# MLP steps of one width (512 columns) and a new written-out issue order, in a kernel for windowed attention and two MLP layers

## The chip, the cores and the metric

The kernel runs on one core of a Trainium2 chip. Times are device microseconds (us). The kernel before takes 620.37 us (median of 3 runs, 620.18 to 620.58). One profiled execution took 622.03 us, of which its trace spans 620.2 us. TensorE is called PE below (PEld is its weight load), VectorE DVE, ScalarE ACT, GpSimd POOL, and the queue that starts the DMAs is SyncE's, SP.

## What is computed

Attention over 2 batches, 8 heads, 768 tokens and head size 64, and then two MLP layers over all 1536 tokens (d_model 512, d_ff 2048):

```
k_sum = max of k, v_sum = mean of v over blocks of 32 tokens (24 blocks)
scores = concat(q k^T / 8 where |i-j| < 16, else -1e9;  q k_sum^T / 8 + log 32)
x = softmax(scores) @ concat(v, v_sum)            -> 1536 tokens x 512
h = x @ w_in ;  y = (h * clip(h+3, 0, 6) / 6) @ w_out      layer 0
h = y @ w_in2;  out = (h * sigmoid(h)) @ w_out2            layer 1
```

All of it is float32. For the MLPs every operand is split in a high and a low part, and each product is three matmuls: high by high, high by low, low by high.

## The kernel before

**Attention.** A unit is 64 query tokens of one batch, all 8 heads; there are 24. A unit goes through `keys` (the 96 near keys and 24 block maxima are copied together, on POOL or DVE), `scores` (PE), `masked` (DVE: adds the mask, finds the maximum), `exps` and `guard` (ACT), `inverse` (DVE), `normal` (POOL or DVE), `turn` (PE transposes), `turned` (copy), `mix` (PE, times the values), `mixed_hi` and `mixed_lo` (the two parts of x). Ahead of that, k and q come in tiles of 256 tokens: `load`, `par` (a copy that puts even and odd tokens apart, one half on DVE and one on ACT), `tr` (PE transposes, two per tile), `k_copy`, `k_max`, `q_copy` out of PSUM. All block maxima of a batch must be there before its first `keys`.

**Weights.** Each of 64 half slices of weights (512 KB) is fetched and rounded to its high and low part: `conv_mag` (ACT), `conv_low`, `conv_clamp`, `conv_join`, `conv_sign` (DVE), `conv_hi` (ACT or DVE), `conv_lo` (POOL or DVE).

**MLP.** The hidden dimension is cut into 16 slices of 128, eight in each half of a layer. A step is one slice f for one chunk of tokens: `hidden i` (12 matmuls in two parts of 6), `act` (ACT), `gate` (DVE), `gate_hi`, `gate_lo` (the two parts of the gated values), `project i` (12 matmuls into 4 PSUM banks, which gather the chunk's output over eight steps). Chunks are 512 tokens (`WIDE`). Only the first chunk of layer 0, half 0 has eight steps of 256 tokens among its steps: slices 0 to 3, each for the tokens of units 0 to 3 and for those of units 4 to 7. So the kernel before has 100 steps. There are 8 PSUM banks in turn, one buffer for `act`'s result (`r`; two more come with `grow 4`), two for the gated values (`g`).

**What sets the order.** The string `ORDER` is the whole program, about 1800 entries, one call each; every engine runs its own share of it strictly in that order, and a `*` puts an operation on DVE that would else be on ACT or POOL. Waits between engines follow from the tiles. `rouse` and `warm` are matmuls whose results nobody uses.

Of the kernel before, what the change touches and what calls it, by code (L numbers as in the profile page):

```python
# [87 lines left out]
1, load k 1 0, k_copy 0 1 0, tr k 0 2 0, k_max 0 2 0, q_copy 0 0 0 1*, tr q 0 2 1, q_copy 0 2 1 0, tr q 0 2 0,
warm 10, par k 0 0, k_max 0 2 1, par k 0 1, tr k 0 0 1, k_copy 0 0 1, tr k 0 0 0, k_max 0 0 1, q_copy 0 2 1 1,
k_copy 0 0 0, tr k 1 0 0, conv_lo 1, k_copy 0 2 0, table 1, warm 0, tr k 1 0 1, q_copy 0 2 0 1, k_max 0 0 0,  # L90
keys 3, k_copy 1 0 1, k_copy 1 0 0, k_max 1 0 0, k_max 1 0 1, fetch 2, conv_low 2, scores 3, masked 3, keys 1,
scores 1, masked 1, keys 2, conv_mag 2, conv_clamp 2, exps 3, guard 3, exps 1, scores 2, keys 0, scores 0,
# [5 lines left out]
7, keys 11, scores 11, guard 7, normal 0, load v 0 2, v_sums 0 2, v_add 0 1, inverse 2, turn 0, exps 5, guard
5, normal 2, load k 1 2, conv_sign 3, v_add 0 2, v_rows 0, conv_join 3, v_put 0 1, turned 0*, v_add 1 0,
load_v 1, tr k 1 2 1, k_copy 1 2 1, k_max 1 2 1, keys 4, scores 4, v_put 0 0*, inverse 5, v_put 0 3, turn 2,  # L100
turned 2, tr k 1 2 0, k_copy 1 2 0, inverse 7, masked 4, k_max 1 2 0, mix 1, v_put 0 2, exps 4, guard 4,
conv_lo 2, keys 9, load k 1 1, mixed_hi 1*, mixed_lo 1, scores 9, tr k 1 1 1, load_v 0, tr k 1 1 0, k_copy 1 1
0, masked 6, normal 5, exps 6, k_max 1 1 1, turn 5, k_copy 1 1 1*, keys 8, guard 6, fetch 4, conv_low 4,
conv_sign 4, mix 0, mixed_hi 0*, mixed_lo 0, scores 8, inverse 6, k_max 1 1 0, turned 5, inverse 4, keys 10,
scores 10, load_v 2, mix 2, conv_mag 4, conv_clamp 4, load_v 3, mixed_hi 2, mixed_lo 2, unstage, normal 7, mix
3, mixed_hi 3, mixed_lo 3, turn 7, turned 7, normal 6, turn 6, conv_hi 3, conv_lo 3, turned 6, conv_join 4,
conv_hi 4, load q 1 0, hidden 0 0, hidden 0 1, act 0, masked 9, tr q 1 0 1, masked 10, q_copy 1 0 1 0, q_copy
1 0 1 1*, tr q 1 0 0, q_copy 1 0 0 1, fetch 5, conv_mag 5, hidden 1 0, hidden 1 1, conv_lo 4*, hidden 2 0,
q_copy 1 0 0 0, act 1, gate 0, gate_hi 0, load q 1 2, tr q 1 2 1, conv_low 5, conv_sign 5, q_copy 1 2 1 0,
gate 1, gate_hi 1, conv_clamp 5, conv_join 5, keys 13, scores 13, q_copy 1 2 1 1, normal 4, turn 4, tr q 1 2  # L110
0, turned 4, fetch 6, conv_low 6, conv_mag 6, keys 12, q_copy 1 2 0 0, conv_sign 6, q_copy 1 2 0 1, conv_clamp
6, conv_join 6, conv_hi 5, masked 11, gate_lo 0, gate_lo 1, conv_hi 6, hidden 2 1, conv_lo 6, project 0 0,
project 1 0, load_v 4, mix 4, mixed_hi 4, mixed_lo 4, act 2, load_v 6, mix 6, gate 2, mixed_hi 6, mixed_lo 6,
load_v 5, mix 5, masked 8, mixed_hi 5, mixed_lo 5, exps 9, guard 9, load_v 7, mix 7, hidden 3 0, hidden 3 1,
act 3, project 0 1, project 1 1, mixed_hi 7*, mixed_lo 7, gate_hi 2*, hidden 5 0, hidden 5 1, gate 3, gate_hi
3*, inverse 9, conv_lo 5, keys 15*, fetch 8, conv_low 8, gate_lo 3*, exps 10, gate_lo 2, guard 10, fetch 7,
conv_mag 7, conv_clamp 7, conv_low 7, conv_sign 7, conv_join 7, hidden 4 0, hidden 4 1, act 5, gate 5, exps 8,
inverse 10, normal 9, guard 8, inverse 8, turn 9, turned 9, project 2 0, project 2 1, hidden 6 0, hidden 6 1,
load_v 9, masked 13, gate_hi 5, conv_hi 7, conv_lo 7*, mix 9, project 3 0, project 3 1, conv_mag 8, conv_clamp
8, conv_sign 8, exps 13, guard 13, mixed_hi 9*, mixed_lo 9, conv_join 8, inverse 13, act 4, gate 4, fetch 11,  # L120
gate_hi 4*, gate_lo 4*, normal 8, turn 8, gate_lo 5, project 5 0, exps 11, guard 11, project 5 1, conv_hi 8*,
turned 8, act 6, gate 6, gate_hi 6, gate_lo 6*, load v 1 1, v_pair 1 1, v_sums 1 1, normal 13, turn 13, turned
13*, hidden 7 0, hidden 7 1, act 7, gate 7, gate_hi 7, scores 12, masked 12, fetch 9, conv_mag 9, conv_low 9,
conv_sign 9, exps 12, project 4 0, conv_clamp 9, guard 12, scores 15, fetch 10, masked 15, exps 15, conv_lo 8,
guard 15, conv_join 9, conv_hi 9*, conv_low 10, conv_sign 10, hidden 8 0, hidden 8 1, load q 1 1, inverse 12,
normal 10, load v 1 2, turn 10, turned 10, gate_lo 7, project 7 0, conv_mag 10, conv_clamp 10, load_v 8, mix
8, project 4 1, act 8, gate 8, inverse 11, keys 14, project 7 1, v_add 1 1, v_pair 1 2, v_sums 1 2, v_add 1 2,
# [834 lines left out]
```

## Time and profile before

| | |
|---|---|
| median of 3 runs | 620.37 us |
| profiled execution | 622.03 us |
| its span in the trace | 620.2 us |
| PE busy | 603.6 us, 97% |
| DVE busy | 406.8 us, 66% |
| ACT busy | 240.3 us, 39% |
| POOL busy | 100.4 us, 16% |
| chain that ended last | PE 90%, DVE 4%, ACT 3%, DMA 1% |

Read the shares by stretch, not over the whole span: the first 120 us hold all of the attention and much of the weight conversion, and there several engines are near full; after that PE alone has no pause. A matmul's listed duration is longer than the distance to the next one, since matmuls overlap; what a matmul costs is the distance from start to start.

### The profile page before, as it was taken

Reading aid. Unit: us, or ns where it says so; the run is one execution under the profiler, and the core shown is the slowest. Engines: PE = TensorE matmul, PEld = TensorE weight load, DVE = VectorE, ACT = ScalarE, POOL = GpSimd, SP = SyncE. Lnnn points to the kernel's source line nnn. Section 1 sums busy time; section 2 is a strip of 40 time slices with the busy share of each in tenths; the row PEclk is TensorE's granted clock in tenths of the full one; section 3 lists DMA queues with packets and bytes.
Section 4 is the critical chain, followed back from the end, with each engine's and each line's share of the span. In section 5 each row is a group of like instructions: output and inputs, shape, how many; then the busy total and the mean of one; then the engine's idle time right before and its main releaser. Section 6 shows DMA issues by size and latency. Waiting matters only on the chain.

```text
span 620.2 us, 8857 instructions
## 1 busy us (share of the span) xinstructions
PE 603.6 (97%) x3324; PEld 506.6 (82%) x3324; DVE 406.8 (66%) x895; ACT 240.3 (39%) x574; POOL 100.4 (16%) x113
## 2 busy tenths in 40 slices
PE   6699999999999999999999999999999999999997
PEld 5688988788888888888888888888888888888886
DVE  5869999876757678567659688435266766423333
ACT  5779967464434224233223243222232243101120
POOL 2564562031102012100003101000000010000000
PEclk9989999999999999999999999999999999999999
DMA  9979393421322223222203222202012220100101
GB/s 250 286 152 238 124 219 91 129 62 45 95 63 98 79 91 94 77 68 63 73 1 102 63 73 73 64 0 70 0 35 81 89 68 1 51 18 1 68 1 68
DMA packets 69050, 51.56 MB, mean 83 GB/s; under 512 B 36368, under 2 KB 63504, under 8 KB 69008
## 3 DMA queue, kind: packets, MB, share of 16 engines
q1 hardware_dynamic: 69008, 51.01, 30.3%
q8 instruction: 26, 0.43, 0.3%
q14 instruction: 16, 0.13, 0.1%
...
## 4 chain that ended last, share of the span: by engine, by line
PE 90%; DVE 4%; ACT 3%; DMA 1%; issue 1%; SPq 0%; POOL 0%; ACTq 0%; POOLq 0%
PE bank L688 41%; PE bank L762 21%; PE bank L759 20%; PE bank L580 3%; PE bank L649 2%; PE bank L637 2%; DMA stage<-in_q_dram 1%; ACT early_w L508 1%; DVE bits L410 1%; DVE bits L403 1%; ACT kT L483 1%; ACT early_w L609 0%; PE bank L524 0%; PE bank L475 0%; DVE bits L390 0%
## 5 line engine op out<-in xcount | busy, mean ns | idle before, releaser
L688 PE MATMUL bank<-x,w 128*128 128x512 f32 (+1 forms) x1008 | 231.3, 381 | 0.4 <-DVE w L425 0.3
L688 PEld LDWEIGHTS bank<-x,w 128*128 128x128 f32 x1008 | 182.6, 188 | 36.3 <-DVE w L425 0.5
L759 PE MATMUL bank<-g,w 128*128 128x512 f32 (+1 forms) x624 | 141.3, 376 | 0.0
L762 PE MATMUL bank<-w,g 128*128 128x512 f32 (+1 forms) x600 | 135.7, 381 | 0.0
L762 PEld LDWEIGHTS bank<-w,g 128*128 128x128 f32 x600 | 109.6, 188 | 21.8
L759 PEld LDWEIGHTS bank<-g,w 128*128 128x128 f32 x624 | 110.3, 188 | 20.7 <-DVE g L736 0.2
L425 POOL TENSOR_TENSOR w<-bits,w 128x512 fp32r<-128x512 f32 x38 | 51.0, 1347 | 353.5 <-ACT w L421 196.7
L736 DVE TENSOR_TENSOR g<-r,g 128x512 fp32r<-128x512 f32 (+1 forms) x95 | 66.9, 709 | 29.2 <-ACT g L730 26.3
L726 DVE TENSOR_TENSOR r<-bank,r 128x512 f32<-128x512 f32 x48 | 32.9, 688 | 65.9 <-ACT r L716 65.7
L716 ACT ACTIVATE r<-bank 128x512 f32<-128x512 f32 x48 | 28.1, 596 | 112.3 <-PE bank L688 109.8
L385 ACT ACTIVATE mag<-words 128x512 f32<-128x512 f32 x64 | 43.0, 671 | 27.6 <-DVE bits L403 20.1
L722 DVE SCALAR_TENSOR_TENSOR r<-r,bank 128x512 f32<-128x512 f32 (+1 forms) x52 | 33.1, 641 | 27.6 <-ACT r L714 27.1
L714 ACT ACTIVATE r<-bank 128x512 f32<-128x512 f32 (+1 forms) x52 | 29.0, 563 | 53.6 <-PE bank L688 42.4
L410 DVE SCALAR_TENSOR_TENSOR bits<-words,bits 128x512 uint32<-128x512 uint32 x64 | 48.5, 758 | 1.3
L403 DVE SCALAR_TENSOR_TENSOR bits<-mag,bits 128x512 uint32<-128x512 uint32 x64 | 47.2, 737 | 1.6
L421 ACT CAST w<-bits 128x512 fp32r<-128x512 f32 x40 | 24.7, 620 | 57.0 <-DVE bits L403 56.9
L688 PE MATMUL bank<-x_late,w 128*128 128x512 f32 x192 | 44.8, 389 | 0.0
L688 PEld LDWEIGHTS bank<-x_late,w 128*128 128x128 f32 x192 | 36.0, 188 | 7.5
L730 ACT CAST g<-r 128x512 fp32r<-128x512 f32 (+1 forms) x43 | 25.4, 594 | 36.0 <-PE bank L762 16.4
L397 DVE TENSOR_SCALAR mag<-mag 128x512 f32<-128x512 f32 x64 | 31.6, 493 | 9.0 <-ACT mag L385 8.8
L730 DVE CAST g<-r 128x512 fp32r<-128x512 f32 (+1 forms) x57 | 28.8, 505 | 11.9 <-PE bank L762 8.3
L609 ACT ACTIVATE early_w<-early_w,stat 128x120 f32<-128x120 f32 x72 | 27.5, 387 | 13.5 <-DVE stat L595 13.5
...
## 6 DMA issues: line engine op xcount, KB each, us to landing
...
```

The lines of the kernel that those rows point to most:

```text
L385: nc.scalar.activation(out=out, in_=low_high(h)[:, 1].bitcast(F32), func=AF.Abs, scale=EXP_SHIFT)
L397: nc.vector.tensor_scalar(out=mag, in0=mag, scalar1=MAG_MIN, scalar2=MAG_MAX, op0=ALU.max, op1=ALU.min)
L403: nc.vector.scalar_tensor_tensor(out=bits, in0=mags.use(h).bitcast(U32), scalar=3, in1=bits, op0=ALU.logical_shift_left, op1=ALU.bitwise_or,)
L410: nc.vector.scalar_tensor_tensor(out=bits, in0=low_high(h)[:, 1], scalar=0x80000000, in1=bits, op0=ALU.bitwise_and, op1=ALU.bitwise_or,)
L425: eng.tensor_tensor(out=w_half(h, 1), in0=bitss.use(h).bitcast(F32), in1=w_half(h, 0).bitcast(F32), op=ALU.subtract,)
L688: nc.tensor.matmul(ps[:, :n], w[:, a, kk * P : (kk + 1) * P], x[:, o // SUB : (o + n) // SUB, b, kk, :], start=(m == 0), stop=(m == last),)
L722: nc.vector.scalar_tensor_tensor(out=r, in0=r, scalar=6.0, in1=ps, op0=ALU.min, op1=ALU.mult)
L726: nc.vector.tensor_tensor(out=r, in0=ps, in1=r, op=ALU.mult)
L730: copier("gate_hi", i)(out=g[:, 0, cols], in_=rs.use(slot(i)[0])[:, cols])
L736: eng.tensor_tensor(out=g[:, 1, cols], in0=r[:, cols], in1=g[:, 0, cols].bitcast(F32), op=ALU.subtract)
L759: nc.tensor.matmul(ps[:, o : o + n], lhs, g[:, b, shift : shift + n], **flags)
L762: nc.tensor.matmul(ps[:, : len(cols)], g[:, a, rows], rhs, **flags)
```

## The change

The eight steps of 256 tokens become four of 512, so that there are 96 steps, and `ORDER` is another string: other places for nearly every entry, other choices of `*`, four `warm` entries for five. Nothing else differs; line numbers fall by 7.

```diff
-FIRST_STEPS = (
-    [(c, 1, f) for c in range(2) for f in range(4)]
-    + [(0, 2, f) for f in range(4, HALF)]
-    + [(c, 2, f) for c in (2, 4) for f in range(HALF)]
-)
+FIRST_STEPS = [(c, 2, f) for c in range(0, 6, 2) for f in range(HALF)]
...
+0, keys 3, conv_clamp 0, q_copy 0 1 0 0, conv_join 0, scores 3, masked 3, exps 0, keys 1*, scores 1, k_copy 0
...
```

The transfers, first. SP's queue at the start of the kernel before (`stage` and `early_w` are tiles of k, q and v, `words` are weights, the first `cst` has the identity, the second the masks):

```order
L433 DMA stage_80<-in_k_dram 128x8x128
L874 DMA cst<-in_consts_dram 128x176
L377 DMA words_69<-in_moe_w_in_dram 128x4x256
L433 DMA stage_81<-in_q_dram 128x8x128
L433 DMA stage_82<-in_k_dram 128x8x128
L377 DMA words_70<-in_moe_w_out_dram 128x1024
L448 DMA early_w_88<-in_q_dram 128x8x64 x2
L433 DMA stage_83<-in_k_dram 128x8x128
L448 DMA early_w_88<-in_k_dram 128x8x64 x2
L874 DMA cst<-in_consts_dram 128x360
```

and the same queue with the change:

```order
L426 DMA stage_80<-in_k_dram 128x8x128
L867 DMA cst<-in_consts_dram 128x176
L426 DMA stage_81<-in_k_dram 128x8x128
L426 DMA stage_82<-in_q_dram 128x8x128
L426 DMA stage_83<-in_k_dram 128x8x128
L441 DMA early_w_88<-in_q_dram 128x8x64 x2
L370 DMA words_69<-in_moe_w_in_dram 128x4x256
L867 DMA cst<-in_consts_dram 128x360
L370 DMA words_70<-in_moe_w_out_dram 128x1024
```

The third k tile of batch 0 was the eighth transfer and is the fifth; the weights have moved behind the tiles of k and q.

DVE next, from its sixth instruction in the kernel before (`bits`, `mag` and `words` belong to the weights' conversion, L461 is `par`, L489 `k_max`, L506 `q_copy`):

```order
L461 COPY stage_81<-stage_81 128x512
L390 TENSOR_SCALAR bits_67<-words_69 128x512
L410 SCALAR_TENSOR_TENSOR bits_67<-words_69,bits_67 128x512
L397 TENSOR_SCALAR mag_66<-mag_66 128x512
L403 SCALAR_TENSOR_TENSOR bits_67<-mag_66,bits_67 128x512
L425 TENSOR_TENSOR w_85<-bits_67,w_85 128x512
L461 COPY stage_82<-stage_82 128x512
L390 TENSOR_SCALAR bits_68<-words_70 128x512
L397 TENSOR_SCALAR mag_66<-mag_66 128x512
L410 SCALAR_TENSOR_TENSOR bits_68<-words_70,bits_68 128x512
L403 SCALAR_TENSOR_TENSOR bits_68<-mag_66,bits_68 128x512
L421 CAST w_85<-bits_68 128x512
```

and with the change, from its seventh (L454 is `par`, L482 `k_max`, L476 `k_copy`, L499 `q_copy`, L588 the first `masked`):

```order
L454 COPY stage_82<-stage_82 128x512
L482 TENSOR_REDUCE kmax_104<-bank_74 128x2x8
L476 COPY kT_98<-bank_75 128x2x256
L482 TENSOR_REDUCE kmax_104<-bank_75 128x2x8
L454 COPY stage_83<-stage_83 128x512
L482 TENSOR_REDUCE kmax_104<-bank_77 128x2x8
L482 TENSOR_REDUCE kmax_104<-bank_73 128x2x8
L499 TENSOR_SCALAR early_w_89<-bank_78 64x8x64
L499 TENSOR_SCALAR early_w_90<-bank_79 64x8x64
L383 TENSOR_SCALAR bits_67<-words_69 128x512
L403 SCALAR_TENSOR_TENSOR bits_67<-words_69,bits_67 128x512
L588 ISA early_w_95,stat_100<-bank_77,cst 128x120
```

Two conversions stood ahead of the first `masked`, and two instructions of one are left there.

Last, PE around its first `hidden` in the kernel before (L649 is `mix`, L637 `turn`, L475 `tr`, L688 `hidden`, L580 `scores`):

```order
L649 MATMUL bank_73<-early_units 64x64 x8
L649 MATMUL bank_78<-early_units 64x64 x8
L637 MATMUL bank_79<-cst,early_units 120x128 x4
L637 MATMUL bank_75<-cst,early_units 120x128 x4
L688 MATMUL bank_73<-x_0_64,w_85 128x256 x12
L475 MATMUL bank_78<-cst,early_w_88 128x128 x4
L475 MATMUL bank_79<-cst,early_w_88 128x128 x4
L688 MATMUL bank_75<-x_0_64,w_86 128x256 x12
```

and with the change (L642 is `mix`, L630 `turn`, L573 `scores`, L681 `hidden`, L468 `tr`):

```order
L642 MATMUL bank_78<-early_units 64x64 x8
L642 MATMUL bank_74<-early_units 64x64 x8
L630 MATMUL bank_75<-cst,early_w_95 120x128 x4
L642 MATMUL bank_73<-early_g_96,early_r_97 64x64 x8
L573 MATMUL bank_77<-early_units,early_w_89 128x120 x4
L681 MATMUL bank_78<-x_0_64,w_85 128x512 x12
L468 MATMUL bank_79<-cst,early_w_88 128x128 x4
L468 MATMUL bank_74<-cst,early_w_88 128x128 x4
L681 MATMUL bank_73<-x_0_64,w_86 128x512 x12
```

The first `hidden` is 512 wide now and stands behind eight `mix` in place of four.

## Rows read from the trace of the kernel before

**Rows 1.** Stretches: length, busy us of PE, PEld, DVE, ACT, POOL, granted clock.

```profile
0.00:52.40 52.40, 40.59 (x369) 36.02 (x369) 37.20 (x130) 36.34 (x111) 23.24 (x44) 0.93 1.00 231
5.06:23.70 18.64, 11.38 (x92) 10.15 (x91) 13.68 (x25) 11.82 (x21) 4.87 (x12) 1.00 1.20 289
23.70:52.40 28.70, 25.20 (x263) 21.86 (x261) 23.35 (x105) 23.23 (x89) 13.89 (x22) 0.88 0.96 207
...
30.00:40.00 10.00, 10.00 (x100) 8.58 (x100) 6.25 (x35) 7.71 (x38) 5.34 (x9) 0.69 0.60 126
50.00:110.00 60.00, 57.69 (x557) 52.13 (x558) 56.42 (x184) 48.17 (x148) 29.65 (x31) 1.00 0.67 160
52.40:80.00 27.60, 25.91 (x271) 24.55 (x272) 25.95 (x85) 23.97 (x78) 14.77 (x16) 1.00 0.65 164
180.00:617.00 437.00, 437.00 (x1977) 362.73 (x1976) 263.47 (x450) 124.22 (x217) 38.26 (x28) 1.00 0.17 55
```

**Rows 2.** Chain that ended last: start, us, what.

```profile
314.71 13.60 PE bank L688 x60
...
603.23 13.86 PE bank L762 x75
```

**Rows 3.** PE in order of time: start, duration, line, shape, count, [idle before].

```profile
9.16 1.17 PE L475 MATMUL bank<-cst,stage 128*128 128x128 f32 x8 [2.23 <-DVE stage L461]
...
20.92 1.15 PE L580 MATMUL bank<-early_units,early_w 128*128 128x120 f32 x8 [1.10 <-POOL early_units L573]
...
24.59 1.04 PE L475 MATMUL bank<-cst,early_w 128*128 128x128 f32 x8
25.46 1.06 PE L880 MATMUL bank<-cst 128*128 128x128 f32 x8
28.65 0.63 PE L637 MATMUL bank<-cst,early_units 128*120 128x128 f32 x4 [2.14 <-DVE stat L624]
...
52.37 1.81 PE L688 MATMUL bank<-x,w 128*128 128x256 f32 x12
...
62.07 0.69 PE L649 MATMUL bank<-early_g,early_r 120*64 120x64 f32 x16
62.59 0.64 PE L649 MATMUL bank<-early_units 120*64 120x64 f32 x16
...
68.11 3.04 PE L688 MATMUL bank<-x,w 128*128 128x256 f32 x24
70.99 0.60 PE L637 MATMUL bank<-cst,early_w 128*120 128x128 f32 x4
...
79.67 0.65 PE L637 MATMUL bank<-cst,early_w 128*120 128x128 f32 x4 [0.76 <-POOL early_w L629]
```

**Rows 4.** DVE in order of time, same columns.

```profile
5.06 0.43 DVE L461 COPY stage<-stage 128x512 f32<-128x512 f32 x1 [4.06 <-DMA stage<-in_k_dram]
...
23.70 0.27 DVE L595 CUSTOM_DVE_ANT_0 early_units<-bank,cst 128x120 f32<-128x120 f32 x1
...
25.32 0.42 DVE L397 TENSOR_SCALAR mag<-mag 128x512 f32<-128x512 f32 x1
...
32.71 0.29 DVE L535 COPY early_w<-bank 128x128 f32<-128x128 f32 x1 [1.81 <-PE bank L524]
```

**Rows 5.** ACT in order of time: `par` of the third k tile, batch 0.

```profile
16.03 0.62 ACT L461 COPY stage<-stage 128x512 f32<-128x512 f32 x1 [0.51 <-DMA stage<-in_k_dram]
```

**Rows 6.** DVE by line and shape: name, count, busy us, mean ns, idle before.

```profile
L489 DVE TENSOR_REDUCE kmax<-bank 128x16 f32<-128x512 f32 x12 | 8.1, 686 | 4.1 <-ACT kT L483 4.1
...
L672 DVE TENSOR_TENSOR x<-bank,x 128x256 fp32r<-128x256 f32 x16 | 6.6, 420 | 1.1 <-ACT x L668 0.7
```

**Rows 7.** Page, the engines' instructions by line, same columns.

```profile
L736 DVE TENSOR_TENSOR g<-r,g 128x512 fp32r<-128x512 f32 (+1 forms) x95 | 66.9, 709 | 29.2 <-ACT g L730 26.3
...
L722 DVE SCALAR_TENSOR_TENSOR r<-r,bank 128x512 f32<-128x512 f32 (+1 forms) x52 | 33.1, 641 | 27.6 <-ACT r L714 27.1
L714 ACT ACTIVATE r<-bank 128x512 f32<-128x512 f32 (+1 forms) x52 | 29.0, 563 | 53.6 <-PE bank L688 42.4
...
L410 DVE SCALAR_TENSOR_TENSOR bits<-words,bits 128x512 uint32<-128x512 uint32 x64 | 48.5, 758 | 1.3
```

More of the change, by code (lines that the diff above doesn't have):

```diff
@@ L88 @@
[L88 to L92, printed above, removed]
@@ L98 @@
[L98 to L102, printed above, removed]
@@ L103 @@
[L103 to L127, printed above, removed]
@@ new lines @@
+7, mix 7, mixed_hi 7, load_v 6, mixed_lo 7, mixed_lo 4, mix 6, mixed_hi 6, turn 9, keys 10, conv_lo 2,
+mixed_lo 6, load_v 5, mix 5, mixed_hi 5, scores 10, mixed_lo 5, fetch 4, conv_low 4, masked 10, conv_hi 3,
+conv_lo 3, k_copy 1 0 1, conv_mag 4, conv_clamp 4, conv_sign 4, turned 9, hidden 0 0, conv_join 4, hidden 0 1,
+exps 8, guard 8, load k 1 2, inverse 8, tr k 1 2 0, k_max 1 2 0, v_add 1 2, tr k 1 2 1, act 0, gate 0, gate_hi
+0*, gate_lo 0, conv_hi 4, hidden 1 0, conv_lo 4*, fetch 5, conv_low 5, conv_sign 5, hidden 1 1, exps 11,
@@ new lines @@
+conv_low 11, gate_lo 4, turned 12, conv_clamp 11, turn 13, conv_sign 11, conv_lo 9*, scores 14, conv_join 11,
+fetch 15, conv_hi 11, conv_low 12, conv_lo 11, conv_mag 12, conv_sign 12, masked 14, turned 13, hidden 5 1,
+masked 15, act 5, gate 5, tr q 1 2 0, q_copy 1 2 0 0, project 4 0, exps 15, guard 15, tr q 1 2 1, grow 0,
+conv_clamp 12, keys 17, gate_hi 5*, gate_lo 5, load_v 13, mix 13, mixed_hi 13, fetch 14, conv_low 14, keys 16,
+q_copy 1 2 1 0, conv_join 12, conv_hi 12, scores 17, q_copy 1 2 1 1, project 5 0, project 5 1, normal 11*,
@@ new lines @@
+12, gate_lo 6, conv_low 15, normal 14, turn 14, turned 14, turn 10, turned 10, conv_sign 15, hidden 7 1,
+masked 16, keys 18*, act 7, mix 14, scores 18, conv_join 15, inverse 17, exps 16, gate 7, conv_hi 15, load_v
+11, mix 11, mix 10, mixed_hi 10, mixed_hi 11, guard 16, conv_hi 13*, conv_lo 13*, project 6 0, project 6 1,
+gate_hi 7*, mixed_lo 10, fetch 16, conv_mag 16, gate_lo 7, conv_lo 15*, project 7 0, load_v 17, finish 0 0 0
+0, finish 0 0 0 1, project 7 1, finish 0 0 0 3, fetch 20, inverse 16, normal 16, conv_low 16, mixed_lo 11,
@@ new lines @@
+17, act 9, gate 9, exps 21, guard 21, hidden 10 0, hidden 10 1, inverse 21, normal 21*, gate_hi 9, gate_lo 9,
+grow 1, turned 18, conv_sign 17, load_v 19, mix 19, conv_mag 17, conv_clamp 17, conv_join 17, conv_hi 17*,
+turn 21, turned 21, mixed_hi 19, mixed_lo 19, hidden 13 0, keys 20, scores 20, masked 20, scores 23, conv_lo
+16*, masked 23, fetch 18, conv_low 18, hidden 13 1, conv_mag 18, act 10, exps 20, exps 23, gate 10, hidden 12
+0, conv_sign 18, guard 20, inverse 20, project 8 0, project 8 1, guard 23, mixed_lo 17, conv_clamp 18,
@@ new lines @@
+conv_join 18, hidden 12 1, conv_lo 17, project 9 0, project 9 1, gate_hi 10, gate_lo 10, keys 22*, scores 22,
+act 11, gate 11, grow 2, conv_hi 18, fetch 19, conv_mag 19, normal 20*, turn 20, conv_low 19, load_v 21,
+load_v 18, masked 22, exps 22, guard 22, project 10 0, mix 18, project 10 1, gate_hi 11*, gate_lo 11, project
+11 0, act 12, gate 12, mix 21, mixed_hi 18*, project 11 1, gate_hi 12*, mixed_lo 18, gate_lo 12, project 12 0,
+inverse 22, act 13, gate 13, gate_hi 13, gate_lo 13, hidden 14 0, hidden 14 1, turned 20*, load_v 20, mix 20,
```

340 lines of the change are left out of this document (173 added, 167 removed).

## The prediction

> **What bounds the kernel now.** I read the page's shares first, then the stretches, the chain that ended last, and PE and DVE in order of time. From 180 us on PE has no pause: 437.0 of 437 us busy at full clock [rows 1]. There the chain is PE alone, in pieces like 60 matmuls in 13.60 us, or 226.7 ns per matmul of 512 columns, up to 603.23 + 13.86 = 617.1 us [rows 2]. So what happens on the other engines there costs nothing, and the end is set by how much matmul work is left when PE stops waiting. Each microsecond that PE loses early is one at the end.
>
> It loses them before its first `hidden` at 52.37 us [rows 3]: `scores` starts only at 20.92, `rouse` and `warm` fill gaps, and the clock falls. From 30 to 40 us the granted clock is 0.69 on average [rows 1]; with the two levels 1.2 and 2.4 GHz that is 6.2 us at the lower one, or 3.1 us of matmul time. From 52.4 to 80 us PE is still idle for 27.60 - 25.91 = 1.7 us [rows 1], the longest pause 0.76 us [rows 3].
>
> Behind PE's waits there stands DVE. Of the first 52.4 us it is busy 37.2 [rows 1]. The 15.2 idle ones are 4.9 until the first tile lands at 5.06, 18.64 - 13.68 = 5.0 from there to the first `masked` at 23.70, and 28.70 - 23.35 = 5.3 after it [rows 1, 4]; of these last the longest pause, 1.81, waits for matmuls at the low clock [rows 4]. From 50 to 110 us DVE is 94% busy (56.42 of 60) [rows 1]: near its limit.
>
> **The change, part by part.** The sum is made against the profiled execution: span 620.2 us, 1.8 more around it (622.03), which I leave as they are; the difference then goes onto the median of 620.37.
>
> *(a) Width.* Eight steps of 24 matmuls with 256 columns become four of 24 with 512. A run of 24 narrow ones goes from 68.11 to 70.99, 120.0 ns each [rows 3]. So 192 x 120.0 = 23.0 us become 96 x 226.7 = 21.8: -1.3 us, all on PE's path. What is saved is a fixed cost: 512 columns at 2.4 GHz are 213.3 ns, the row has 13 more. The Trainium skill ("TensorE: Matmul & The Clock Gate", section "Wait — 56ns, not 53.3ns?") puts it at about 2.5 ns per matmul; by that the saving would be 96 x 2.5 ns = 0.2 us, an estimate. The rows measure this kernel's own pairs of weight load and matmul, so they decide.
>
> *(b) The head.* Three things move. The third k tile of batch 0 was the eighth transfer, reached at 16.03 us [rows 5], and becomes the fifth. Two weight conversions leave the stretch ahead of the first `masked` on DVE. And the first `hidden`, 512 wide, now needs units 0 to 7, not 0 to 3.
>
> First `masked`: at some 2 us per transfer (16.03 / 8) the tile lands at 10 instead of 16 us. In the kernel before 7.7 us pass from the tile to the first `masked`, partly because conversions stand between. With all of the 7.7 it comes at 17.7, without 1.2 us of it at 16.5; I take 17.2. Until then, counted from the first `par`, DVE has 16 instructions in place of 25 that took 13.68 us [rows 1], so 8.8 us: its idle time there is 17.2 - 5.1 - 8.8 = 3.3, not 5.0.
>
> First `hidden`: counted over both orders up to the last `mixed_lo` that it needs, DVE has three `masked` more (two of them take 23.70 to 25.32, 0.81 each [rows 4]: +2.4), four `mixed_lo` more (0.42 each [rows 6]: +1.7) and four `k_max` fewer (0.69 each [rows 6]: -2.8). The rest (a conversion less, two `keys` and a `v_pair` taken over from POOL) I count as even. So 37.2 + 1.3 = 38.5 us of DVE work. Idle: 4.9 + 3.3 + late pauses. Late ones were 5.3, in part the low clock's; the new order has longer attention chains ahead of `hidden`, but more units in flight to fill them. None would be the best, 5.3 the same; I take the middle, 2.7. That gives 38.5 + 4.9 + 3.3 + 2.7 = 49.4 us for the first `hidden`. ACT's share up to there, 36.3 us now [rows 1], changes by two operations and stays below DVE's, and POOL with 23.2 has room.
>
> PE has by then also done more: four `mix` (62.07 to 62.59, 0.52 each [rows 3]) and two `turn` more, four `tr` less (24.59 to 25.46 holds two, 0.44 each [rows 3]; `turn` has as many matmuls): 2.1 + 0.9 - 1.8 = +1.2 us that need not be done later. Gain of the head: 52.4 - 49.4 + 1.2 = 4.2 us. Bounds: no late pause and `masked` at 16.5 give 46.0 and a gain of 7.6; all idle time as before gives 38.5 + 15.2 = 53.7 and a gain of -0.1.
>
> *(c) The first chunk's eight steps.* After the head PE asks for more sooner, and DVE, 94% busy there, has conversions to do that the kernel before had behind it. This loss the trace doesn't show directly. At best the 1.7 us of pauses go (-1.7). At worst each of the eight steps ends with a pause like the longest there now, 0.76 us: +6.1. I take +2.0, nearer the small pauses, because PE has transposes, `scores`, `turn` and `mix` of 16 units to lay between.
>
> *(d) The rest.* Layer 0's later chunks, layer 1 and the last `close` hold the same matmuls in another order. In PE's present 437 us without pause DVE is busy 263 and ACT 124 [rows 1], so moved conversions and DMAs hide. At the end four parts of `project`, 24 matmuls or 5.4 us, lie between the last `hidden` and `close`, over a chain of `act`, `gate`, a cast and `gate_lo` of about 0.6 + 0.6 + 0.6 + 0.7 = 2.5 us [rows 7]. Zero; without that cover it would be those 2.5 us.
>
> Sum: -1.3 - 4.2 + 2.0 = -3.5 us. Span 616.7, profiled execution 618.5, median 620.4 - 3.5 = 616.9 us. With all bounds at one end: 620.4 - 1.3 - 7.6 - 1.7 = 609.8 and 620.4 - 1.3 + 0.1 + 6.1 = 625.3.
>
> **Rivals.**
>
> *Head and first chunk both smooth.* `hidden` at 47, no loss in (c): -1.3 - 5.4 - 1.2 = -7.9, so 612.5 us. For it: DVE's longest pause in the present head follows a slow clock. Against: ACT is busy 36.3 of 52.4 us too, and two engines that loaded, each in strict order, seldom run without waits.
>
> *The clock falls again.* It fell after PE's pause of 2.14 us that ended at 28.65; an earlier one of 2.23, ended at 9.16, was followed by no fall [rows 3, 1]. In the new order `scores 1` waits for `keys 1` on DVE, which stands behind three `masked` and two pieces of a conversion, some 3.6 us, while PE has two `scores` of about 1 us: it will wait about 2 us again. If the clock then halves, the pauses come back, `hidden` starts at 53.7, and the sum is -1.3 + 0.1 + 2.0 = +0.8: 621.2, no change that can be told. The Trainium skill ("TensorE: Matmul & The Clock Gate", section "What's actually happening") says that the low clock is the default and only activity lifts it. The trace agrees for the second pause and not for the first, so I don't take the fall for certain.
>
> *Slower: the single `r` buffer starves PE.* Until `grow 4` there is one buffer for `act`'s result, and the next step's `act` waits for `gate_lo`. At 512 columns that chain is 2.5 us [rows 7], and where DVE puts the pieces of a conversion into it (three at up to 0.76 us [rows 7]) some 4.8. PE's cover per step is the next `hidden`, 2.7 us, and 1 to 2 us of attention. If a step loses 1 us, eight lose 8: -1.3 - 4.2 + 8 = +2.5, so 622.9. It decides from 0.84 us per step on (6.7 in all, which takes the sum to +1.2). Against it: of the 2.3 us that PE idles from 50 to 110 us, 1.7 lie before 80 [rows 1], so at most 0.6 fall where steps of 512 already run on the same buffer.
>
> **How the numbers follow.** Forecast 0.58, own range 614.5 to 619.1; smooth 0.14; clock 0.15; starved 0.13. A difference under 0.2% (1.24 us) is about what can't be told from none. The forecast and the smooth case are faster, and a little of the clock case, where a fall is short: 0.73. The rest of the clock case and the mild end of the starved one make "same" 0.15; slower 0.12. The range reaches from the smooth case to the edge of the starved one: 612.4 to 621.8.
>
> **What would show it.** First `masked` near 17 us, first `hidden` near 49 to 50 and a granted clock of 1.00 up to there would show (b) right; a stretch at 0.50 after the third `scores` would show the second rival. For (c), PE's idle time from the first `hidden` to 110 us: under 4 us for the forecast, over 8 with `act` behind `gate_lo` for the starved case. (a) needs 226.7 ns per matmul in all MLP runs. The forecast is wrong if the first `hidden` comes after 53 us, or if PE pauses anywhere after 180 us.

## The result, and the profile after

The changed kernel takes 612.58 us (median of 4 runs, 612.36 to 613.91) beside 620.48 us for the kernel before: ratio 0.9875, 95% interval 0.9857 to 0.9892, or -7.9 us. Forecast were 616.9 us and -3.5; the time lies inside the range of 612.4 to 621.8 by 0.2 us, the gain is more than twice the forecast one. The profiled execution took 612.76 us, its span is 611.0. A few executions, those profiled for the control and for the twelve doubled signs among them, ran disturbed (859 to 862 us at a granted clock near 0.65 from end to end, or 1363 and 2990 us) and are left out of every median.

The stretches of the changed kernel (columns as in [rows 1]: length, busy us of PE, PEld, DVE, ACT, POOL, granted clock, DMA share, GB/s):

```profile
0.00:52.40 52.40, 45.45 (x457) 39.64 (x458) 42.34 (x171) 40.08 (x135) 30.96 (x46) 0.97 1.09 244
5.06:23.70 18.64, 14.04 (x99) 13.01 (x99) 14.97 (x50) 12.31 (x35) 4.77 (x12) 0.91 1.19 284
23.70:52.40 28.70, 27.40 (x343) 22.62 (x342) 27.20 (x121) 26.48 (x100) 21.71 (x24) 1.00 1.11 233
30.00:40.00 10.00, 9.79 (x143) 8.01 (x143) 9.18 (x39) 9.82 (x38) 8.13 (x10) 1.00 1.09 219
50.00:110.00 60.00, 60.00 (x433) 50.03 (x432) 55.86 (x156) 49.94 (x146) 13.39 (x18) 1.00 0.75 186
52.40:80.00 27.60, 27.60 (x174) 22.84 (x173) 25.48 (x66) 24.70 (x70) 8.61 (x11) 1.00 0.91 217
```

Against [rows 1] every engine does more in the first 52.4 us (DVE 42.3 us for 37.2, POOL 31.0 for 23.2), the clock stays at 1.00 from 30 to 40 us, and from 52.4 to 80 us PE is busy 27.60 of 27.60 us, where it had been 25.91. DVE is as loaded as before there (25.48 for 25.95).

PE in order of time (start, duration, line, shape, count, [idle before and who ended it]), for [rows 3]:

```profile
9.81 0.65 PE L468 MATMUL bank<-cst,stage 128*128 128x128 f32 x4 [0.44 <-DVE stage L454]
11.95 2.15 PE L468 MATMUL bank<-cst,stage 128*128 128x128 f32 x12 [1.48 <-DVE stage L454]
...
16.29 1.05 PE L573 MATMUL bank<-early_w,early_w 128*128 128x120 f32 x8
...
19.30 1.15 PE L573 MATMUL bank<-early_units,early_w 128*128 128x120 f32 x8 [1.06 <-POOL early_units L566]
21.83 2.04 PE L573 MATMUL bank<-early_w,early_w 128*128 128x120 f32 x16 [1.39 <-DVE early_w L566]
...
48.48 2.98 PE L681 MATMUL bank<-x,w 128*128 128x512 f32 x12
51.30 1.03 PE L468 MATMUL bank<-cst,early_w 128*128 128x128 f32 x8
52.09 3.02 PE L681 MATMUL bank<-x,w 128*128 128x512 f32 x12
```

`scores` starts at 16.29 us (20.92 before), the first `hidden` at 48.48 (52.37), and behind it no line has an idle time. The wait for `keys 1`, at which the prediction's rival of the falling clock let it fall, is there (1.39 us ahead of 21.83) and no fall follows it in this execution. A fall stands elsewhere: the twelve transposes behind the pause of 1.48 us take 2.15 us, and from 12.8 to 16.1 us the clock is 0.50:

```profile
12.80:16.10 3.30, 3.30 (x18) 3.30 (x17) 2.46 (x4) 1.67 (x3) 0.93 (x3) 0.50 1.08 371
```

The third k tile on ACT, for [rows 5], and the first `masked` on DVE, for [rows 4]:

```profile
10.94 0.62 ACT L454 COPY stage<-stage 128x512 f32<-128x512 f32 x1 [0.74 <-DMA stage<-in_k_dram]
```

```profile
17.48 0.28 DVE L588 CUSTOM_DVE_ANT_0 early_w<-bank,cst 128x120 f32<-128x120 f32 x1 [0.15 <-PE bank L573]
```

The tile is there at 10.94 us (16.03; 10 forecast), `masked` at 17.48 (23.70; 17.2 forecast). The chain that ended last, for [rows 2], is PE alone from the first `hidden` on, in the same 226.7 ns per matmul (5.44 us for 24) where the MLP's matmuls stand together; one piece ahead of it is new, a transfer of v that PE waits for twice, 0.45 and 0.38 us:

```profile
40.92 5.90 DMA early_r<-in_v_dram
...
243.79 5.44 PE bank L681 x24
```

Three groups of the page, for [rows 7] (count, busy us, mean ns, idle before):

```profile
L729 DVE TENSOR_TENSOR g<-r,g 128x512 fp32r<-128x512 f32 x96 | 66.4, 699 | 28.5 <-ACT g L723 25.4
...
L403 DVE SCALAR_TENSOR_TENSOR bits<-words,bits 128x512 uint32<-128x512 uint32 x64 | 44.7, 698 | 1.0
...
L715 DVE SCALAR_TENSOR_TENSOR r<-r,bank 128x512 f32<-128x512 f32 x48 | 32.5, 683 | 14.0 <-ACT r L707 13.8
```

The operations of a step cost what they cost (0.70 for 0.71 us; 0.68 for 0.68 at 512 columns, since the 0.64 of [rows 7] has eight `gate` of 256 columns among its 52); the waits ahead of them are DVE's and not PE's.

**Where the time went.** A PE that never waits behind its first `hidden` needs a time from there to the end that only its own instructions set. So each trace falls into two parts, the start of the first `hidden` and the rest of the span:

| trace | first `hidden` | rest | span |
|---|---|---|---|
| before | 52.37 | 567.8 | 620.2 |
| after | 48.48 | 562.5 | 611.0 |
| difference | -3.9 | -5.3 | -9.2 |

The 5.3 us of the rest: width -1.3 as forecast; matmuls that now stand ahead of the first `hidden`, by the traces' counts behind it (64 fewer `mix`, 8 `turn` and 16 for the sums of v, 16 more `tr`; at the distances in the trace of before, -2.1 - 0.9 - 0.7 + 1.8) -1.9; pauses -1.7; and -0.4 that these don't explain. The traces differ by 9.2 us and the medians by 7.9, because the profiled execution of before (622.03 us) lay 1.6 us above the median of 620.48 and that of after 0.2 above its own.

### The profile page after: what moved, and what is told of

Read it like the earlier page. It is cut to its first block, busy times and chain, and to the rows that moved or that the text cites. A ratio compares the mean times of both kernels' runs of the same rounds, so it can differ in the third digit from the quotient of the medians.

```text
span 611.0 us, 8649 instructions
## 1 busy us (share of the span) xinstructions
PE 600.7 (98%) x3224; PEld 499.4 (82%) x3224; DVE 402.4 (66%) x912; ACT 240.3 (39%) x570; POOL 67.4 (11%) x84
## 4 chain that ended last, share of the span: by engine, by line
PE 95%; DVE 2%; ACT 1%; DMA 1%; issue 0%; ACTq 0%
PE bank L681 43%; PE bank L752 22%; PE bank L755 21%; PE bank L573 3%; PE bank L642 2%; PE bank L630 1%; PE bank L468 1%; DMA early_r<-in_v_dram 1%; PE bank L883 1%; ACT early_units L602 0%; DVE kmax L482 0%; PE bank L536 0%; PE bank L873 0%; ACT early_w L501 0%; ACT early_w L602 0%; DVE early_w L588 0%
## 5 line engine op out<-in xcount | busy, mean ns | idle before, releaser
L681 PE MATMUL bank<-x,w 128*128 128x512 f32 x960 | 230.8, 391 | 0.0
L681 PEld LDWEIGHTS bank<-x,w 128*128 128x128 f32 x960 | 179.0, 188 | 37.1 <-DVE r L719 0.5
L752 PE MATMUL bank<-g,w 128*128 128x512 f32 x576 | 138.3, 392 | 0.0
L729 DVE TENSOR_TENSOR g<-r,g 128x512 fp32r<-128x512 f32 x96 | 66.4, 699 | 28.5 <-ACT g L723 25.4
L709 ACT ACTIVATE r<-bank 128x512 f32<-128x512 f32 x48 | 27.8, 596 | 119.4 <-PE bank L681 118.9
L418 POOL TENSOR_TENSOR w<-bits,w 128x512 fp32r<-128x512 f32 x23 | 31.5, 1371 | 361.4 <-DVE w L414 218.3
L707 ACT ACTIVATE r<-bank 128x512 f32<-128x512 f32 x48 | 28.5, 597 | 57.8 <-PE bank L681 48.9
L723 ACT CAST g<-r 128x512 fp32r<-128x512 f32 x49 | 30.2, 621 | 48.0 <-PE bank L755 21.7
L403 DVE SCALAR_TENSOR_TENSOR bits<-words,bits 128x512 uint32<-128x512 uint32 x64 | 44.7, 698 | 1.0
L681 PE MATMUL bank<-x_late,w 128*128 128x512 f32 x192 | 45.0, 389 | 0.0
L681 PEld LDWEIGHTS bank<-x_late,w 128*128 128x128 f32 x192 | 36.0, 188 | 7.5
L715 DVE SCALAR_TENSOR_TENSOR r<-r,bank 128x512 f32<-128x512 f32 x48 | 32.5, 683 | 14.0 <-ACT r L707 13.8
L723 DVE CAST g<-r 128x512 fp32r<-128x512 f32 x47 | 20.5, 436 | 18.0 <-PE bank L755 14.0
L418 DVE TENSOR_TENSOR w<-bits,w 128x512 fp32r<-128x512 f32 x41 | 27.9, 689 | 1.5 <-ACT w L414 0.7
```

The lines of the kernel that those rows point to most:

```text
L403: nc.vector.scalar_tensor_tensor(out=bits, in0=low_high(h)[:, 1], scalar=0x80000000, in1=bits, op0=ALU.bitwise_and, op1=ALU.bitwise_or,)
L418: eng.tensor_tensor(out=w_half(h, 1), in0=bitss.use(h).bitcast(F32), in1=w_half(h, 0).bitcast(F32), op=ALU.subtract,)
L681: nc.tensor.matmul(ps[:, :n], w[:, a, kk * P : (kk + 1) * P], x[:, o // SUB : (o + n) // SUB, b, kk, :], start=(m == 0), stop=(m == last),)
L715: nc.vector.scalar_tensor_tensor(out=r, in0=r, scalar=6.0, in1=ps, op0=ALU.min, op1=ALU.mult)
L723: copier("gate_hi", i)(out=g[:, 0, cols], in_=rs.use(slot(i)[0])[:, cols])
L729: eng.tensor_tensor(out=g[:, 1, cols], in0=r[:, cols], in1=g[:, 0, cols].bitcast(F32), op=ALU.subtract)
```

## The experiments

The time given first for each experiment is a median, with the range in brackets; the medians of the kernel before, measured beside them, are 620.6 to 620.9 us. For the changed kernel its seven undisturbed runs are the base: 612.31 to 613.91, median 612.8.

**The width.** Every matmul of layer 0, half 0 of the changed kernel cut in two of 256 columns, 576 more instructions in the same order:

```diff
+            if i < 3 * HALF:
+                for part_n in range(2):
+                    nc.tensor.matmul(
+                        ps[:, part_n * SUB : (part_n + 1) * SUB],
+                        w[:, a, kk * P : (kk + 1) * P],
+                        x[:, part_n, b, kk, :],
...
```

> The changed kernel, with each matmul of the 24 steps of layer 0, half 0 issued as two of 256 columns into the same bank: 576 matmuls become 1152, nothing else changes. By the price of the rows (120.0 ns against half of 226.7) PE needs 576 x 13.3 ns = 7.7 us more: about 620.3. If width costs only some 2.5 ns per matmul (rival), 1.4 us more: about 614.

620.0 us (619.6 to 620.9): +7.2, or 12.5 ns per matmul added. Its first `hidden` and what follows:

```profile
49.69 3.12 PE L683 MATMUL bank<-x,w 128*128 128x256 f32 x24
52.65 1.03 PE L468 MATMUL bank<-cst,early_w 128*128 128x128 f32 x8
```

24 narrow ones take 2.96 us where 12 wide ones took 2.82 (48.48 to 51.30), 11.7 ns per matmul added. Part of the 7.2 us is the clock's: this trace has a fall that costs 1.2 us of first `hidden` (below). Its rest alone, 569.0 us for 562.5, gives 6.5 us or 11.3 ns. The Trainium skill ("TensorE: Matmul & The Clock Gate", section "Wait — 56ns, not 53.3ns?") has about 2.5 ns of fixed cost per matmul; by an estimate from it the split would cost 576 x 2.5 ns = 1.4 us. In this stream, with a weight load for each matmul, the trace doesn't agree, and step (a), with 13.3 ns, had nearly the right size.

**The clock.** First the kernel before with ten more filler matmuls in the pause of 2.14 us after which its clock fell (`warm 5`) [rows 3]:

```diff
-        for _ in range(2):
+        for _ in range(12 if i == 5 else 2):
```

> The kernel before, with 12 filler matmuls in place of 2 in the fifth warm, which lies in PE's pause from 26.5 to 28.65 us. If the low clock after that pause is what slows the head (first theory), the clock stays at 1.00 from 29 to 36 us, DVE's late pauses shrink from 5.3 us to about 3, the first hidden comes at 50 us, and the time falls by 2 to 3 us to about 618. If the order on DVE and ACT sets the pace (rival), the first hidden stays at 52 us and the time within 0.6 us of 620.5.

619.15 us (619.09 to 619.62), ratio 0.9984 (0.9974 to 0.9994), -1.5 us. In its trace the clock is 1.00 throughout; the first `hidden` comes at 49.51, but the rest is 567.9, pauses included:

```profile
49.51 1.82 PE L688 MATMUL bank<-x,w 128*128 128x256 f32 x12
```

```profile
30.00:40.00 10.00, 9.96 (x124) 8.57 (x122) 8.32 (x39) 8.79 (x40) 7.70 (x12) 1.00 0.82 180
52.40:80.00 27.60, 25.92 (x275) 24.63 (x274) 25.84 (x72) 22.53 (x75) 14.82 (x15) 1.00 0.65 163
```

So the fall is worth 1.5 us of the median, and 2.9 us of first `hidden` in the trace of before. The kernel before shows the same by itself: three of its 56 executions beside these experiments had a mean clock of 1.00 and took 619.06 to 619.42 us. Not every fall costs time, though: with the fillers, executions at a mean clock of 0.994 took 619.09 to 619.62 us, and those at 1.00 took 619.09 to 619.20. The changed kernel has a fall of its own; to see how often, it was run again unchanged:

> The changed kernel once more, unchanged, beside the next three on one chip. In the traces of three of its variants the clock halved from about 21 to 27 us, behind the wait for keys 1, and not from 12.8 to 16.1 as in its own trace. If that second place is open to the kernel itself, its times fall into two groups, 612.4 to 612.8 and some 1 to 1.5 us above; if the variants brought it about, all runs are 612.4 to 612.8 us.

612.31, 613.15 and 613.16 us: apart by 0.85, a little less than expected. Of all seven runs four lie at 612.3 to 612.8 and three at 613.2 to 613.9, but their mean clocks (0.994 to 0.997) don't sort them, so two groups are not shown. But four traces, its own and those of three variants, have the same instructions up to the first `hidden` and differ there in where the clock falls and in the waits that go with it: 47.28 us without a fall (`a_less_chunk` below), 48.48 with the fall from 12.8 us on (its own), 49.69 and 49.88 with one from 21 to 27 us at `keys 1` (the split one, and `a_sign_half` below). First the row of the 47.28, then how the fall at `keys 1` looks in the trace of `a_mag_head` below:

```profile
47.28 3.02 PE L684 MATMUL bank<-x,w 128*128 128x512 f32 x12
```

```profile
18.47 1.15 PE L574 MATMUL bank<-early_units,early_w 128*128 128x120 f32 x8 [1.04 <-POOL early_units L567]
21.34 3.77 PE L574 MATMUL bank<-early_w,early_w 128*128 128x120 f32 x16 [1.72 <-DVE early_w L567]
```

```profile
20.00:27.00 7.00, 5.66 (x26) 5.67 (x27) 5.95 (x33) 6.66 (x27) 2.46 (x4) 0.54 1.15 292
```

16 `scores` in 3.77 us instead of 2.04. Then fillers in the pauses of the changed kernel, `warm 9` and within `scores` into its own bank:

```diff
-0, k_copy 0 2 0*, tr q 0 0 1, q_copy 0 0 1 1, k_max 0 2 0, par k 1 0, tr k 0 1 1, k_max 0 1 1, tr q 0 0 0,
+0, k_copy 0 2 0*, tr q 0 0 1, q_copy 0 0 1 1, k_max 0 2 0, par k 1 0, warm 9, tr k 0 1 1, k_max 0 1 1, tr q 0
...
+        for _ in range({3: 4, 1: 6}.get(u, 0)):
+            nc.tensor.matmul(ps[:, :P], ident, ident, start=True, stop=True)
...
-        for _ in range(2):
+        for _ in range(6 if i == 9 else 2):
```

> The changed kernel with filler matmuls in TensorE's pauses of the head: warm 9 moved ahead of the transposes of the second k tile with six matmuls in place of two (pause of 1.48 us at 10.5), four ahead of scores 3 (pause of 1.06) and six ahead of scores 1 (pause of 1.39). If the low clock costs this kernel time, it does not fall and the time is 611 to 612 us, less spread than the unchanged one; if VectorE paces the head whatever TensorE's clock is, the time is 612.4 to 612.8; if the fillers come in the way, 613 or more.

611.68 us (611.55 to 614.05), ratio 0.9862 (0.9842 to 0.9882): three runs at clock 1.00 near 611.6, one at 614.05. The latter is the profiled one, with a new pause and a fall behind it:

```profile
43.60 0.69 PE L644 MATMUL bank<-early_g,early_r 120*64 120x64 f32 x16 [2.46 <-DMA early_r<-in_v_dram]
```

```profile
45.00:48.00 3.00, 3.00 (x44) 2.49 (x36) 2.33 (x12) 1.73 (x4) 1.48 (x1) 0.52 1.14 288
```

On top of the fillers, the values of unit 4 fetched earlier:

```diff
-2, turn 5, turned 5, normal 6, load k 1 0, masked 9, turn 4, turned 4, tr k 1 0 1, exps 9, conv_clamp 3, load
-v 1 2, k_max 1 0 1, tr k 1 0 0, load_v 4, k_max 1 0 0, turn 7, turned 7, v_pair 1 2, mix 4, guard 9, inverse
+2, turn 5, turned 5, normal 6, load_v 4, load k 1 0, masked 9, turn 4, turned 4, tr k 1 0 1, exps 9,
+conv_clamp 3, load v 1 2, k_max 1 0 1, tr k 1 0 0, k_max 1 0 0, turn 7, turned 7, v_pair 1 2, mix 4, guard 9,
```

> The filler version (fillers ahead of the transposes of the second k tile, scores 3 and scores 1) and besides the transfer of unit 4's values moved ahead of the k tile of batch 1, since the filler version waited 2.46 us for these values before its mix 4 at 43.60 us. If TensorE's pauses in the head cost time by themselves, the wait goes and the time is 610 to 611.2 us; if the conversions on VectorE set the first hidden anyway, it stays at the filler version's 611.6 us; if the k tile of batch 1, now later, is waited for, 612 or more.

614.16 us (611.84 to 614.75), ratio 0.9898 (0.9882 to 0.9914): one run at 1.00 with 611.84, three with a fall (mean clock 0.997) at 614.1 to 614.8. Its trace is the undisturbed one: no wait for the values, first `hidden` at 47.55, rest 562.6. Where the clock fell in the three others is not recorded. The filler version is about 1 us faster than the changed kernel as long as the clock holds, but the intervals overlap, so no version is shown to beat it.

**The head.** The changed kernel with `conv_sign` issued twice for pieces 0 to 3, 2.4 us more DVE work, and in a kernel of its own `conv_mag`, 2.3 us more ACT work, both with this loop around the instruction:

```diff
+        for _ in range(2 if h < 4 else 1):
```

> The changed kernel with the same instruction issued twice for weight pieces 0 to 3: four more, 2.4 us more VectorE work ahead of the first hidden. If VectorE paces the head, as the prediction's part (b) says, the first hidden comes about 2.4 us later (50.9 instead of 48.5 us) and the time is 612.6 + 2.4 = 615 us. If the chain of scalar operations and transfers paces it, the first hidden stays within 0.5 us and the time is 612.6 to 613.4 us.

> The counterpart on ScalarE: the changed kernel with the first instruction of the conversion (Abs, 128x512, about 0.6 us) issued twice for weight pieces 0 to 3, 2.3 us more ScalarE work ahead of the first hidden. If VectorE alone paces the head, the time stays within 1 us of 612.6. If ScalarE paces it with VectorE, each in its place, it grows by 1 to 2.3 us (613.6 to 614.9 us).

615.88 us (614.70 to 616.39), and 614.8 (614.71 to 614.98). Both traces have the fall behind `keys 1`, so the 49.8 us above is their base: first `hidden` at 51.91 (+2.1 for 2.4 us of DVE) and at 50.57 (+0.8 for 2.3 us of ACT). The rests are 562.7 and 562.4, as in the changed kernel. So added work on DVE delays the head nearly in full and on ACT only in part; of the 2.0 us that ACT's work cost in the median, 1.2 are the other place of the fall. The mirror image, `conv_sign` left out for these pieces:

```diff
+        if h < 4:
+            words.use(h)
+            return
```

> The changed kernel without the sign instruction for weight pieces 0 to 3 (their signs are left out of the result): 2.4 us less VectorE work ahead of the first hidden, the mirror image of the doubled ones. If VectorE paces the head, the first hidden comes 1.5 to 2.4 us earlier and the time is 610 to 611 us, if the first chunk can follow. If the first chunk then asks for conversions too soon, what is won in the head comes back as pauses there and the time is 612 us or more.

612.67 us (612.57 to 613.28), no gain. First `hidden` at 47.93, with a fall from 21 to 24 us; the rest is 563.0, with a pause of 0.29 us for a k tile of batch 1. What was won in the head, 0.55 us against the changed kernel's own trace, didn't reach the end. One of its runs had a clock of 1.00 throughout and took 612.66 us all the same, so the fall isn't what held this kernel; how much a fall hides in its head is open. Next the order of transfers:

```diff
-k 0 0, tr k 0 0 1, k_copy 0 0 1*, tr k 0 0 0, load k 0 2, par k 2 0, warm 3, k_max 0 0 1, par k 2 1, load q 0
+k 0 0, tr k 0 0 1, k_copy 0 0 1*, tr k 0 0 0, fetch 0, load k 0 2, par k 2 0, warm 3, k_max 0 0 1, par k 2 1,
+load q 0 0, k_max 0 0 0, tr k 0 2 1, par q 0 0, par q 0 1, k_max 0 2 1, k_copy 0 0 0, fetch 1, load k 0 1, par
...
```

> The changed kernel with the transfers of weight pieces 0 and 1 put back ahead of the third and the second k tile of batch 0, so that the third k tile is the sixth of SP's transfers and not the fifth; all else stays. If the order of the transfers carries the early masked, each 512 KB transfer ahead costs about 2 us: first masked at 19 to 21 us instead of 17.5 and 614 to 616.5 us. If VectorE's work carries the first hidden whatever the start, 612.4 to 613.4 us.

616.08 us (615.70 to 617.51): +3.3. The third tile on ACT and the first `masked` on DVE:

```profile
13.56 0.62 ACT L454 COPY stage<-stage 128x512 f32<-128x512 f32 x1 [2.06 <-DMA stage<-in_k_dram]
```

```profile
20.13 0.28 DVE L588 CUSTOM_DVE_ANT_0 early_w<-bank,cst 128x120 f32<-128x120 f32 x1
```

2.6 us later each, and the first `hidden` 3.0 later, at 51.46. So the head's gain hangs on the order of the transfers, in part by way of the clock, which in this trace falls twice. The reverse, in the kernel before, made it slower twice. Transfers and conversions 0 and 1 were moved behind the third tile and the first two `masked` (first form), or behind `scores 0` with conversion 2 (second form):

```diff
+q_copy 0 0 1 0, tr k 0 2 1, k_copy 0 2 1, fetch 0, fetch 1, load k 1 0, k_copy 0 1 0, tr k 0 2 0, k_max 0 2 0,
...
+fetch 2, conv_low 2, scores 3, masked 3, keys 1, scores 1, masked 1, conv_mag 0, conv_low 0, conv_sign 0,
+conv_clamp 0, conv_join 0, conv_hi 0, conv_lo 0*, conv_low 1, conv_mag 1, conv_clamp 1, conv_sign 1, conv_join
```

```diff
+tr k 0 0 0, k_max 0 0 1, q_copy 0 2 1 1, k_copy 0 0 0, tr k 1 0 0, k_copy 0 2 0, table 1, fetch 0, fetch 1,
...
+scores 0, conv_mag 0, conv_low 0, conv_sign 0, conv_clamp 0, conv_join 0, conv_hi 0, conv_lo 0*, conv_low 1,
```

> The kernel before, with its first two weight transfers behind the third k tile, and their conversions behind the first two masked: only this part of the new order. If the early start of attention makes the gain in the head (first theory), the first masked comes 3 to 4 us earlier, at about 20 us, the first hidden at about 49.5, and the time is about 618. If the conversions are only put off, and PE waits for them later (rival), the first hidden or the pauses after it give it back: 620 to 621.5.

> The kernel before (eight narrow steps, its own order otherwise) with the transfers of weight pieces 0 and 1 moved behind the k and q tiles, and the conversions of pieces 0, 1 and 2 moved behind the scores of units 0 to 3. The third k tile becomes the fifth or sixth transfer. If the earlier tile and the undisturbed first masked are what the head gains by, the first masked comes at 18 to 19 us instead of 23.7 and the time falls by 2 to 4 us, to 616.5 to 618.5. If what matters is the total of VectorE work ahead of the first hidden, the conversions then stand in one block in front of the rest and nothing is won: 620 to 622 us.

631.48 us (630.54 to 631.97) and 626.15 us (625.77 to 628.05). The waits of PE in the first (engine, line, waited for: us in total, times, longest), and in the second:

```profile
PE bank L580 <- POOL early_units L573: 10.7, 1, 10.7
```

```profile
PE bank L637 <- DVE stat L624: 9.4, 1, 9.4
```

The first `masked` comes at 23.83 and 19.67 us, and yet the first `hidden` at 62.34 and 56.27: in one form POOL's `conv_lo 1` stood ahead of the next `keys`, in the other DVE's conversions stood as a block ahead of `inverse 3`, and in strict order all behind them waited. So neither run tells whether the earlier `masked` is worth time in the old order; a move of few entries isn't the new order. The rests, 567.9 and 568.0, are those of the kernel before.

**The first chunk.** `conv_sign` issued twice for pieces 6 to 17 of the changed kernel (7.2 us of DVE), and in a second kernel for 6 to 11 (3.6 us, `h < 12`):

```diff
+        for _ in range(2 if 6 <= h < 18 else 1):
```

> The changed kernel, with conv_sign done twice (the second time changes nothing) for the 12 half slices 6 to 17, which are converted from the first hidden to about 115 us: 12 x 0.6 = 7.2 us more work on DVE there. If DVE is at its limit there, as step (c) had it, PE waits for 4 us or more: 616.6 or above. If DVE runs ahead of PE and the eight steps have cover enough (rival), PE hardly waits: under 613.6, against 612.6 without it.

> The changed kernel with the last instruction of the weight conversion (sign, 128x512 on VectorE, about 0.6 us) issued twice for weight pieces 6 to 11: six more instructions, 3.6 us more VectorE work in the first chunk and none ahead of it. If VectorE is at its limit all through the first chunk, the time grows by all of it: 612.6 + 3.6 = 616.2 us. If there is some slack that the twelve doubled ones used up (they cost 7.0 us for 7.2 us of work), half of them cost less than half: 612.6 to 614.6 us.

619.2 us (618.1 to 622.0), ratio 0.9984 (0.9969 to 1.0000), and 617.2 us (615.9 to 618.2): +6.4 and +4.4 over 612.8. The pauses of PE in the trace of the second:

```profile
67.17 0.63 PE L469 MATMUL bank<-cst,early_w 128*128 128x128 f32 x4 [1.35 <-ACT mag L378]
...
92.19 0.66 PE L469 MATMUL bank<-cst,early_w 128*128 128x128 f32 x4 [0.84 <-DVE stat L589]
```

```profile
50.00:110.00 60.00, 57.51 (x374) 46.56 (x372) 58.73 (x162) 47.58 (x134) 16.02 (x18) 1.00 0.72 177
```

DVE is at 98%, and its rest is 566.3, 3.8 more for 3.6 us of work, of which 2.5 are pauses that the trace lists. The opposite, the signs of pieces 6 to 17 left out, in the changed kernel and in the one before:

```diff
+        if 6 <= h < 18:
+            words.use(h)
+            return
```

> The changed kernel without the sign instruction for weight pieces 6 to 17 (the signs of these weights are left out of the result): 7.2 us less VectorE work in the first chunk, the mirror image of the doubled signs, which cost 7.0 us. If VectorE held TensorE back in the first chunk, as part (c) assumed, the time falls by 1 us or more, to 611.6 or below. If the new order just balances the two engines, so that TensorE loses nothing there, the time stays at 612.4 to 612.8 us.

> The kernel before without the sign instruction for weight pieces 6 to 17 (the signs of these weights are left out of the result), as in the same cut of the changed kernel, which won nothing by it (613.36 us). If VectorE held TensorE back in the first chunk of the kernel before, its 1.7 us of pauses go and the time is 618.5 to 619.5 us. If those pauses had other causes, it stays at 620.3 to 621 us.

613.36 us (612.39 to 613.58): nothing for 7.2 us. And 619.87 us (618.42 to 621.48), ratio 0.9984 (0.9974 to 0.9994) in the kernel before: -0.8. The stretch behind the first `hidden`, of the changed kernel and of the one before, each with the cut:

```profile
52.40:80.00 27.60, 27.23 (x171) 22.40 (x170) 22.21 (x59) 23.78 (x66) 7.64 (x10) 1.00 0.94 225
```

```profile
52.40:80.00 27.60, 26.56 (x280) 25.28 (x279) 24.18 (x81) 23.69 (x78) 15.27 (x17) 1.00 0.75 182
```

The changed kernel's DVE falls from 92% to 80% and PE gains nothing: it had no pause there to lose, and now waits 0.37 us for a k tile's transfer. In the kernel before some 0.6 of the 1.7 us of pauses go. Last the width without the new order: the kernel before, its eight narrow steps merged into four, each entry at the later place of the two (three entries of one step a little earlier):

```diff
-    [(c, 1, f) for c in range(2) for f in range(4)]
-    + [(0, 2, f) for f in range(4, HALF)]
+FIRST_STEPS = [(0, 2, f) for f in (1, 0, *range(2, HALF))] + ...
...
```

> The width alone: the kernel before with its eight steps of 256 columns merged into four of 512, each at the place of the later of its two parts, and the rest of its order kept. By the prediction's parts (a) and (c), width in an order not made for it loses pauses in the first chunk: first hidden at about 54 us (units 0 to 7 are needed), TensorE idle over 3 us from there to 110 us, and 621 to 624 us. If the width carries the gain, 614 to 618 us and hardly a pause behind the first hidden.

632.15 us (630.64 to 632.34), ratio 1.0177 (1.0162 to 1.0192): 11.3 us slower than before, more than expected. PE's longest pauses, and its stretch from the first `hidden` to 110 us:

```profile
52.24 0.55 PE L468 MATMUL bank<-cst,early_w 128*128 128x128 f32 x3 [1.42 <-DMA early_w<-in_q_dram]
...
61.87 7.50 PE L681 MATMUL bank<-x,w 128*128 128x512 f32 x24 [1.89 <-ACT stat L613]
...
75.44 2.80 PE L752 MATMUL bank<-g,w 128*128 128x512 f32 x11 [1.43 <-DVE g L729]
...
92.60 1.88 PE L752 MATMUL bank<-g,w 128*128 128x512 f32 x5 [2.73 <-DVE g L729]
```

```profile
61.87:110.00 48.13, 43.97 (x270) 34.52 (x271) 33.99 (x95) 29.09 (x94) 15.53 (x16) 0.93 0.41 102
```

Units 4 to 7 and their v come too late in this order: the first `hidden` is at 61.87, 9.5 us later than before, the clock falls soon after it (0.50 from 64 to 66 us, 24 matmuls in 7.5 us), and PE is idle 48.13 - 43.97 = 4.2 us from there to 110, in waits of `project` for the gated values (`g`). These 4.2 us are the loss that step (c) feared, and in the new order, at the same width, they are gone; the larger part of the 11.3 us is the late first `hidden`. Which of the new order's moves does it is not shown.

## Why the prediction was wrong

(a) Right in kind and nearly in size: 226.7 ns where the MLP's matmuls stand together, and 11.3 to 12.5 ns per matmul by the split where the step has 13.3: -1.1 to -1.2 us for -1.3.

(b) Nearly right. First `masked` 17.48 for 17.2, first `hidden` 48.48 for 49.4, work done earlier 1.9 us for 1.2 (the step left out the sums of v): -5.8 for -4.2 in the traces. DVE's time up to the first `hidden`, and its parts:

```profile
0.00:48.48 48.48, 41.52 (x436) 36.28 (x437) 38.64 (x157) 36.19 (x122) 29.33 (x44) 0.96 1.09 242
5.06:17.48 12.42, 10.27 (x70) 9.61 (x70) 8.90 (x17) 6.12 (x11) 1.43 (x4) 0.86 1.19 291
17.48:48.48 31.00, 27.25 (x351) 22.66 (x351) 29.58 (x140) 28.78 (x111) 23.42 (x29) 1.00 1.13 236
```

Its work is 38.6 us for the 38.5 counted, its idle time 4.9 + 3.5 + 1.4 for 4.9 + 3.3 + 2.7: what was off are the late pauses, 1.4 where the middle of the bounds, 2.7, had been taken. The sign of a clock at 1.00 up to there didn't come (0.50 from 12.8 to 16.1). Of the 3.9 us by which the first `hidden` comes earlier, part is the clock's: without a fall on either side it is 49.51 against 47.28, so the order itself wins 2.2 us there. DVE as the pace of the head is shown upward (+2.1 for 2.4 us of added work), not downward.

(c) **This step failed.** It put +2.0 us on the first chunk, because "DVE, 94% busy there, has conversions to do that the kernel before had behind it". Measured: -1.7, all pauses gone, an error of 3.7 us of the 4.4 between -3.5 and -7.9. The new order doesn't push work into the chunk: DVE has done 42.3 us by 52.4 where it had done 37.2, and from 52.4 to 80 us it has as much as before, 25.5 for 26.0. And a full DVE was taken for a waiting PE. That DVE is near its limit was right: 3.6 us more work cost 3.8. But PE waits only where a value comes after its turn, and in the new order none does, at a DVE share of 92%. In the old order too its load was only part of the pauses: with 7.2 us less of it some 0.6 of the 1.7 us went. The same cut in the new order can't decide this, as no pause was left to win. The step's own fear was real for the width alone (4.2 us of pauses in `b_wide`), so the term mixed two changes: what the width costs in the old order, and what the new order does.

(d) Zero, measured -0.4 at most, not resolved. The remaining terms of the error, 1.6 from (b) and 0.4 here, are mostly offset by the 1.4 us by which the profiled execution of before was further above its median than that of after; that offset is chance.

The rivals. "Smooth" named the right outcome in (c) and the right time (612.5), at 0.14; its first `hidden` at 47 is reached only where the clock doesn't fall. "The clock falls again" at `keys 1` is real in six of the variants' traces, but costs 1.2 us of first `hidden` against the fall that the changed kernel's own trace has, not 4.3. The Trainium skill ("TensorE: Matmul & The Clock Gate", section "What's actually happening") has the low clock as the default that activity lifts; the traces agree that a fall follows a pause, and show that which pause it follows differs between executions of the same instructions. "The single `r` buffer" didn't show: no pause behind the first `hidden`.
